# A stored order of work replaced by a newly searched one, with 80 identity products in place of 120

## The chip, the core and the metric

The kernel runs on one core of one Trainium2 chip. The metric is the device time of one launch in microseconds (us). The kernel before has a median of 756.46 us over 3 runs (756.37 to 758.33). TensorE (PE in the rows) multiplies matrices and writes PSUM, VectorE (DVE), ScalarE (ACT) and GpSimd (POOL) work on elements, SyncE (SP) issues DMAs. GpSimd doesn't read PSUM in this kernel: all its operands lie in SBUF.

## The reference

Three networks follow each other; the weights of the last two come as float64.

```
q_assign = argmax(q_n . c_n); k_assign = argmax(k_n . c_n)        # 16 clusters, per head
scores = where(q_assign == k_assign, q k^T / 8, -1e9)             # 2 x 8 heads x 768 x 768
x = softmax(scores) v                                             # to 1536 tokens x 512
h = x @ w_in;  g = h if h >= 1, 0 if h <= -1, else (h+1)^2/4;  x = g @ w_out
out = ((x @ w1) * (x @ w2)) @ w3 @ w_out2
```

## The kernel before

**Stages.** The 1536 tokens are two blocks, one a batch. A block has 4 units (pairs of heads), a unit two halves of 384 queries, a half six scores: 96 scores, s 0 to s 95, each of 128 queries by 768 keys. For a score TensorE multiplies twice into a buffer of PSUM (`s_mm`, line 799: the parts, then the mask); VectorE takes the maximum (line 807), GpSimd scales it (812), ScalarE exponentiates (820). Every score of block 0 and every third of block 1 is then transposed on TensorE (837), the others by DMA. Only when ScalarE and VectorE have copied the result out, or split it into high and low parts (lines 348 to 353), is the PSUM buffer free. After six scores `pv` multiplies with v into the one bank `av` (908, 916), VectorE scales the result there (927, 929) and splits it into X.

While attention runs, float64 weights are turned into floats: ScalarE (1051, 1080), VectorE (1055, 1061, 1067, 1073), GpSimd (1084). w3 and w_out2 are multiplied to one matrix (`wp_mm`, 1142). The dense layers of block 0 (`mm4`, 1198; twelve products of 128x384 a step) run between the scores of block 1; those of block 1 come last, partly by products of quarter matrices (1450). Block 0's scores use four PSUM buffers, block 1's two.

**What sets the order.** Every step is entered in a plan with `add(name, {engine: cost}, due, fn, needs, takes, frees, ..., near)`. `Plan.order` doesn't search: it reads the table `ORDER`, two letters a step, which give the step's number and which of its engines does it, and issues the steps so. Costs, due times and `near` steer only the search that once made the table, which isn't in the file. Each engine executes its instructions in that order and waits by semaphores for tiles. `needs` are only asserted on.

**The identity products.** `idle_mm` (line 460) multiplies the identity matrix with itself into columns 384 to 511 of the bank `av`; nobody reads them. As a writer of the tile `av`, such a product waits for earlier readers of `av`, which later serves as a bank of the dense layers too. There are 120: `N_IDLE` = 90 that come after `c_const`, which makes the identity, and `N_IDLE1` = 30 that come after score 47, the last of block 0. In TensorE's order 50 of them stand ahead of the first score, 21 between the first and the seventh, 49 after the seventh.

**The start.** The centroids are loaded and normed (lines 413 to 442); TensorE multiplies k and q with them (512); VectorE makes masks in four steps, for k and for q (526, 532, 539, 544), TensorE (548) and VectorE (552) end them, and a DMA on ScalarE's queue carries the mask to the first score. Meanwhile q and k are split: high parts on ScalarE or VectorE, low parts (`q_lo`, `k_lo`, line 353) on GpSimd or VectorE.

Of the kernel before, what the change touches and what calls it, by code (L numbers as in the profile page):

```python
# [38 lines left out]
    "###%#*#,#6#(#<#8#:#@#.#0%u(.&y(<#F#D%w(D%y#2%|&#&%&(&*&,&2&|(P(#(0(4(2(,&4(F&8&6(H<8#J#N#L#a#B#_#e#i#X&:&<&>"  # L39
    "&@&B#y$(&.#o#|#m$,#s#c#H$%$6$>#u(>(@&0#4#k&D&F(8<F<:<R((<<(%<a(6(J<H<J<><@(*<T<V<L<N(:<m<B<D(B<c(L$:$H#R#P$R"  # L40
    "#q#Z$F$L$J$_$a$##g$]$D$X$*$m+@+B<]<P=#=2<o+X+D+L+N+P+R+e+g+i+k+F<q<X+Z<e+]<g<Z<i<_$N%#%*%%$q$V$0$Z$e$k$4%(#]"
    "$.$w+T+m+H+K=%+_+a$u%.%6$T=4=6<k=8+V+c+q+s$@$<,#,@=:=<=@=L+o+u+w<w=>,%,(,B,D$o#w$B%2$y$8$P,L$2+y%0,*+|,,,.(N"
    "=(<s=*=,<u=.=0<y$s%4$|,X,Z,](c,N,P,0,2,e,8=B=D=F=N=P=H=R=J=T,F,H=Z,_,R,T$i=g=w(T(V,4,7#T,J,V,q,g,i=V=X=]=i,s"
    ",a-#-%-(,u<|,d,:(^(k(n=_=k(S=m=a,k>0,w,y>@-*(_,<(b,>=o-0,m,o,|-,$g-@$c#V-X-L-Z-.-8=q=s-2-B-D-]=y(Z>2(X-F-e-H"
    "-N-P-R-_=|>4>#>%=c&H>(>*(s-J>:>6=e>8><-T-a-V-c>N>B>_-q-g-i-s-u-k=u>,>.-w>D>F>H>J>L.#.@.B-4-6>q-:.%>P>R-m-y>>"
    "?(?6.(.D>T>V(j>X>Z-o-|.*.0.F.2.L.X.N.P.Z.]>a>c?F-<>e->>s?*.,.H...R.J._>u(r>g?,>w?.>i>k&J).?0?2?4(y(|>]>m>o.e"
    "(e(g?X.T.a.g.i>y(v.4(x.7>|?#.V)%.c?8?@(o.8),/#.q.k.m?i#>?%/%/(?w)(.o.s.u.w/*?:?<?>?B/@/B/D?H?J?Z?k)6/F)#?]?m"
    "?o.:.<?L?N.>/,.y.|/.&L?D?c?T?V)*/H)0/0/2?q?s?P?u?R/L/N/P/R?_?a/K)8?e)4@(@.):?y/8)3/T/4/7/X/Z/]/:/</q/e/g)@/_"
    "/i/s/u@@@P/k/w?g/W?|@#@%@*@0)<@_@B/a0#@o0%0(0*/y/m/o/c@D@2@4@6@F@H@8@:/|@J@L@,@=/>0@0,0B&c&a@>0X0L@i@R@T@V)D"
    ")J)FA(0.@N08@a0D0F0H0N0Z0]0P)M@c)C)Q&e)H&N@X@q0R0_0aA*&g)R%,0T@e@g00@Z@]@s@u@w@yA,@|0JA.A0@k&PA2A402A80V0c)N"  # L50
    "AFAV0e0g0i&R&T0k&i&k&V&mA:A<&o@mA#)>0m0o0q04Ai06Ay0s0u0w0:0<1#1%1(AH1*&qA>A@&XABADAJ0>ALANA60y&s1,0|1.&Z1@1L"
    "1NA%&u&wAPAXAkAZ1P&]&_18B.1RARB>A|1B1D1F10121X1Z1]AmAoA]A_AaAcB#AqB%1_ATAeAg)XB(B*B,1H1T1aAsAu1J1V1c1e1q1sBP"
    "B81416B01g1i1u1wBa1k1:B2B4B6B:2@2#2B2%2(AwB@BR2*20222D1y1m1o1~1<2FBoB<BL)T)V2,2HBBBD1>BFBHBTBN)ZBJ2.BZBVBXB]"
    "2L2N2PBcC%2JByBeBgBiBkBm2RBqBsBuBw2426282T2V2e2X2Z2g2q3#)_B|2i2k2]2_2s2u3%)])h)b)c3(2:)qB_2m)f)jC(GX2w3*3032"
    "2<2>C*)nC,C.C02oC#C4C8CV2y2a2c3,2|3.)sC2C6)l)o34363N%a3PC:C<3R3TCu3V3@3B3D3F)u)w383:CYD:3=3X3>CZ)y)|C>C@CC3H"
    "3J3Z3LCwDX*#CyCDCFDw3]3_3aCJCLCOCH3k3mD<CPCS3c3e3g3iC]C_E<CT3o3qD>CbCcCiCk3y3|4#CeCgEJ3s3u3w4%CnCoCrCs4(4*C|"
    "D#D%D(D.DZDyGuD0D24.4042D]4446D+D,D4D6D@DB4J4L4N4P*%4,484:*(DLDED8D~DFDIDJ4XDNE>E@DQ4R4T4VDRDkDm4<4>DoDqEXD_"
    "4Z4g4iELDaDT**EgEuDd4]4kDVDtDu4_H64a*-*/*04c4eEODe4m4o4qDgDi4s4DEBEDE#E%E)4u4w4y4|E*E-E.E0E2EZE]5*5,5.*2E4E6"
    "5#5%5(4@EFE8F:5052EHE:4C5456585:5<Ei*5*?*@*6*85>*:5@FXGc5B5DH@EcEeE_5c5e5g5i5kEkET5T5V5XEb5F*B5HEPEwEz5mFwF<"
    "EVG<5ZEqEmEREsEoF?4FF[4H*<F^5J5q5s5u*D5]5_5aGJGZG]5MG_GaE|F.FzF|F#F%F(F+6%6(6*5o5w5y5|6#F0GwF2F4GyF7F,G|H#F8"  # L60
# [24 lines left out]
    "]q^u_6]#]4_D^w[o]%[u^C^0]n^D]7]>_F_*]s^o^k]@]B]*],]v_-_8`V].]8];]<^m_L_N^y]0]2_Q]f]E_#^%_I_%]F_;`X_T_J_R[q^q"
# [56 lines left out]
def cluster_attention_moe_kernel(  # L142
# [200 lines left out]
    def f(t):  # L343
        return t.bitcast(F32)
# [298 lines left out]
    def by_copy(u):  # L643
        return u < NP
# [1071 lines left out]
```

## Time and profile before

| | |
|---|---|
| median of 3 runs | 756.46 us |
| profiled execution | 756.23 us |
| its span, first to last instruction | 754.5 us |
| around the span | 1.7 us |
| TensorE, VectorE, ScalarE, GpSimd busy | 97%, 85%, 59%, 40% of the span |
| granted TensorE clock, mean | 0.997 |

The busy shares say which engine has no room left. The granted clock is a share of 2.4 GHz, and 0.5 of it is 1.2 GHz. In a timeline, an idle time in brackets with a name after the arrow is a wait of that engine and who ended it. A record of a matrix product lasts longer than the distance to the next one, since products overlap in the pipeline: what a product costs is read from start to start. Plain float32 products have two records each, so line 460 has 240 records.

### The profile page before, as it was taken

How to read it: one execution, taken by the hardware profiler on the slowest of the kernel's cores; microseconds unless marked ns; L12 is line 12 of the kernel's file. 1: busy time of each engine (PE TensorE's matmuls, PEld its weight loads, DVE VectorE, ACT ScalarE, POOL GpSimd, SP SyncE). 2: the span in 40 equal slices, each digit the busy share in tenths (PEclk: the TensorE clock that was granted, in tenths of full speed). 3: DMA queues.
4: the chain of work that ended last, by engine and by line, in shares of the span. 5: the costliest groups of instructions: out<-in, count | busy, mean ns of one | idle time of the engine just before them, and what ended most of it. 6: DMA issues, size and time to landing. Idle time of an engine off the chain costs nothing.

```text
span 754.5 us, 12341 instructions
## 1 busy us (share of the span) xinstructions
PE 729.9 (97%) x4352; PEld 646.8 (86%) x4353; DVE 638.7 (85%) x1148; ACT 446.8 (59%) x832; POOL 303.0 (40%) x367
## 2 busy tenths in 40 slices
PE   6998999999999999999998999999999999999998
PEld 4975656556599999998998999999899999999997
DVE  5998888988888889999999999759898888899841
ACT  6687887667777867695775665422664444443310
POOL 6242244222343424454354422225561543167711
PEclk9999999999999999999999999999999999999999
DMA  8463565756668767697877785453231303122212
GB/s 291 124 204 111 177 206 201 265 185 200 178 163 190 141 157 189 177 238 192 215 167 204 198 221 148 119 186 120 63 99 29 99 28 99 56 58 69 63 55 92
DMA packets 100973, 112.77 MB, mean 149 GB/s; under 512 B 61488, under 2 KB 69680, under 8 KB 100912
## 3 DMA queue, kind: packets, MB, share of 16 engines
q1 hardware_dynamic: 78768, 52.48, 27.4%
q10 hardware_dynamic: 22144, 59.52, 25.2%
q8 instruction: 34, 0.56, 0.3%
q14 instruction: 27, 0.22, 0.1%
HBM read 73.70 MB, written 20.19 MB: 124 GB/s over the span
## 4 chain that ended last, share of the span: by engine, by line
PE 76%; DVE 13%; ACT 4%; issue 3%; DMA 3%; POOL 0%; ACTq 0%; DVEq 0%; POOLq 0%
PE mo L1198 33%; PE sc L799 7%; PE sc L1450 6%; PE sc L1198 6%; PE mo L1142 4%; PE mo L1450 4%; PE sc L837 4%; PE av L460 3%; PE av L916 3%; PE av L908 2%; PE av L1450 2%; DVE nm L807 2%; DVE wf L1055 1%; ACT pt L348 1%; DVE wf L1067 1%
## 5 line engine op out<-in xcount | busy, mean ns | idle before, releaser
L1198 PE MATMUL mo<-X,whl 128*128 128x384 f32 x900 | 168.8, 341 | 0.0
L1198 PEld LDWEIGHTS mo<-X,whl 128*128 128x128 f32 x900 | 157.2, 190 | 2.0 <-ACT P L820 0.6
L1198 PE MATMUL mo<-G,whl 128*128 128x384 f32 x720 | 133.2, 339 | 0.0
L353 POOL TENSOR_TENSOR whl<-wf,whl 128x512 fp32r<-128x512 f32 x60 | 80.3, 1339 | 130.5 <-ACT whl L348 73.6
L1198 PEld LDWEIGHTS mo<-G,whl 128*128 128x128 f32 x720 | 125.4, 188 | 1.5 <-DVE kq L350 0.3
L807 DVE TENSOR_REDUCE nm<-sc 128x1 f32<-128x768 f32 x96 | 89.8, 950 | 19.2 <-PE sc L799 15.6
L1084 POOL TENSOR_TENSOR wf<-wf,w 128x512 int32<-128x512 int32 x32 | 43.1, 1347 | 74.3 <-ACT w L1080 23.0
L820 ACT ACTIVATE P<-sc,nm 128x768 f32<-128x768 f32 x64 | 57.4, 899 | 23.4 <-POOL nm L812 14.7
L812 POOL TENSOR_SCALAR nm<-nm 128x1 f32<-128x1 f32 x96 | 23.9, 249 | 111.8 <-DVE nm L807 106.3
L799 PE MATMUL sc<-k,q 128*128 128x512 f32 (+1 forms) x192 | 55.2, 369 | 5.9 <-DVE phl L353 4.1
L348 ACT ACTIVATE whl<-wf 128x512 fp32r<-128x512 f32 x70 | 43.7, 627 | 25.5 <-PE mo L1198 9.6
L348 ACT ACTIVATE pt<-sc 128x768 f32<-128x768 f32 (+1 forms) x59 | 46.3, 808 | 20.1 <-PE sc L837 16.0
L1142 PE MATMUL mo<-wo,wf 128*128 128x512 f32 x128 | 57.7, 593 | 0.0
L837 PEld LDWEIGHTS sc<-ident,P 128*128 128x128 f32 x384 | 43.6, 141 | 11.5 <-ACT P L820 5.3
L837 PE MATMUL sc<-ident,P 128*128 128x128 f32 x384 | 49.8, 274 | 2.4 <-ACT P L820 2.3
L799 PE MATMUL sc<-kq 80*128 80x512 f32 (+1 forms) x192 | 49.5, 339 | 0.0
L1051 ACT ACTIVATE wf<-w 128x512 f32<-128x512 f32 x64 | 42.6, 674 | 8.0 <-POOL wf L1084 2.3
L1067 DVE SCALAR_TENSOR_TENSOR wf<-w,wf 128x512 uint32<-128x512 uint32 x64 | 44.1, 691 | 1.2
L1142 PEld LDWEIGHTS mo<-wo,wf 128*128 128x128 f32 x128 | 23.5, 190 | 23.7 <-issue 23.1
L799 PEld LDWEIGHTS sc<-k,q 128*128 128x128 f32 x192 | 31.6, 189 | 14.0 <-DVE phl L353 4.6
L460 PE MATMUL av<-ident 128*128 128x128 f32 x240 | 36.9, 287 | 6.7 <-DVE X L353 2.6
L460 PEld LDWEIGHTS av<-ident 128*128 128x128 f32 x240 | 33.5, 199 | 10.0 <-DVE X L353 2.9
(218 smaller groups left out, 1537.1 us busy)
## 6 DMA issues: line engine op xcount, KB each, us to landing
wf<-wd ACTq DMA_DIRECT2D x64, 256.0 KB, 2.7
w<-in_w_out_dram ACTq DMA_DIRECT2D x24, 512.0 KB, 4.2
wd<-wf SPq DMA_DIRECT2D x48, 256.0 KB, 3.0
w<-in_w3T_dram ACTq DMA_DIRECT2D x16, 512.0 KB, 4.1
w<-in_w_in_dram ACTq DMA_DIRECT2D x16, 512.0 KB, 4.8
w<-in_w_dram ACTq DMA_DIRECT2D x16, 512.0 KB, 4.1
wf<-wp ACTq DMA_DIRECT2D x16, 256.0 KB, 3.1
kq<-in_kT_dram SPq DMA_DIRECT2D x8, 384.0 KB, 5.1
```

The source lines that it names most:

```text
L348: nc.scalar.activation(out=out, in_=in_, func=AF.Copy)
L353: (nc.gpsimd if e == "POOL" else nc.vector).tensor_tensor(out=out, in0=a, in1=b, op=ALU.subtract)
L460: nc.tensor.matmul(BUFS["av"][0][:, TG:TG + 128], ident, ident, start=True, stop=True)
L799: nc.tensor.matmul(ps[:, n], q[0:n_rows, q0:q0 + 128], k[0:n_rows, n], start=first, stop=not first)
L807: nc.vector.tensor_reduce(out=nm, in_=T[("sc", b), s], axis=AX.X, op=ALU.max, negate=True)
L820: nc.scalar.activation(out=new(("P", b), s).rearrange("p n s -> p (n s)") if by_pe(s) else T[("sc", b), s], in_=T[("sc", b), s], func=AF.E ...
L837: nc.tensor.transpose(T[("sc", b), s][:, c], p[:, c], ident)
L1067: nc.vector.scalar_tensor_tensor(out=w, in0=T[w64, i][:, :, 1], scalar=0xC0000000, in1=w, op0=ALU.bitwise_and, op1=ALU.bitwise_or)
L1084: nc.gpsimd.tensor_tensor(out=w, in0=w, in1=T[w64, i].bitcast(I32)[:, :, 0], op=ALU.add)
L1142: nc.tensor.matmul(acc, w[:, k4 * 128:(k4 + 1) * 128], wo2[:, hf * 4 + k4], start=(hf == 0 and k4 == 0), stop=(hf == 1 and k4 == 3),)
L1198: nc.tensor.matmul(acc, w[:, a, k4 * 128:(k4 + 1) * 128], rhs(c, k4), start=(first and k4 == 0 and n == 0), stop=(last and k4 == 3 and n = ...
L1450: nc.tensor.matmul(ps, lhs(av, a, k), rhs(bv, c, k), start=k == 0 and n == 0, stop=k == 1 and n == 2,)
```

## The change

The table is replaced (3134 steps become 3094). The entries that steered the search change with it:

```diff
-    "###%#*#,#6#(#<#8#:#@#.#0%u(.&y(<#F#D%w(D%y#2%|&#&%&(&*&,&2&|(P(#(0(4(2(,&4(F&8&6(H<8#J#N#L#a#B#_#e#i#X&:&<&>"
...
+    "##%%%(%*%:#*#,#%#8#(#4%#%@%>%<#<#@#B&*#.#0#2&8&-#L%,&(&>&;&F&7&D#c#P;@&0#R#6#a;N;Z;i%.#:#k%B&N&P&@#Z$(;J%0%2"
...
-        plan.add(name, engines, due, fn, needs, takes, frees, behind, moves, (near if near and near[0] == ("sc", 0) else None))
+        plan.add(name, engines, due, fn, needs, takes, frees, behind, moves, (near if near and near[0] in (("sc", 0), "av") else None))
...
-    N_IDLE, N_IDLE1 = 90, 30
+    N_IDLE, N_IDLE1 = 80, 0
...
-            add(("idle", after, i), {"PE": 0.22}, 1e4 + i, idle_mm, [(lag + 0.23 * i, after)])
+            add(("idle", after, i), {"PE": 0.22}, 1e4 + i, idle_mm, [(lag + 0.23 * i, after)], near=("av", "cT"))
...
-            add(("am", b, w), {"PE": 1.8}, t + 0.9, a_mm(b, w, range(NP)), ...
+            add(("am", b, w), {"PE": 1.8 if b else 2.4}, t + 0.9, a_mm(b, w, range(NP)), ...
...
-                    [("k2", u, h), ("klo", u, h)] + ([("k2h", u, h), ("q1h", u, h)] + ...
+                    [("k2", u, h), ("klo", u, h)] + ([("idle", "c_const", i) for i in range(N_IDLE)] if s == 6 else []) + ([("k2h", u, h), ("q1h", u, h)] + ...
```

The remaining lines of the diff add `near=` for the bank `av` to `c_T`, `c_put`, the splits of X, `pv` and `xm`. Since the table alone is read, what changes on the chip is the order, the engines of some steps, and 40 products fewer. The table is a line shorter, so code behind it moves up a line: line 799 of before is 798 in the change.

Of the 80 products 50 stand ahead of the first score, 30 between the first and the seventh, none after (before: 50, 21, 49). VectorE has 1112 steps (1107 before), ScalarE 897 (893), GpSimd 345 (354). Counted in the order, VectorE has 390 steps ahead of the maximum of score 66 (378 before) and 591 ahead of that of score 84 (576).

VectorE at the start, before, from the making of k's mask on (`sc` is a PSUM buffer, `P` and `phl` its tiles for masks):

```order
L526 STREAM_TRANSPOSE P_106<-sc_175 128x768
L532 TENSOR_REDUCE amx<-P_106 128x48
L539 TENSOR_TENSOR phl_108<-P_106,amx 128x768
L544 STREAM_TRANSPOSE phl_108<-phl_108 128x768
L526 STREAM_TRANSPOSE P_107<-sc_175 128x768
L532 TENSOR_REDUCE amx<-P_107 128x48
L539 TENSOR_TENSOR phl_109<-P_107,amx 128x768
L544 STREAM_TRANSPOSE phl_109<-phl_109 128x768
L552 TENSOR_SCALAR mask_115<-sc_176 128x768
L552 TENSOR_SCALAR mask_115<-sc_175 128x768
```

and in the change, from the second of two low parts of q on:

```order
L352 TENSOR_TENSOR q_100<-kq_116,kq_103 64x768
L349 CAST k_97<-kq_116 64x768
L525 STREAM_TRANSPOSE P_106<-sc_177 128x768
L531 TENSOR_REDUCE amx<-P_106 128x48
L538 TENSOR_TENSOR phl_108<-P_106,amx 128x768
L543 STREAM_TRANSPOSE phl_108<-phl_108 128x768
L525 STREAM_TRANSPOSE P_107<-sc_177 128x768
L551 TENSOR_SCALAR mask_115<-sc_178 128x768
L531 TENSOR_REDUCE amx<-P_107 128x48
L538 TENSOR_TENSOR phl_109<-P_107,amx 128x768
L543 STREAM_TRANSPOSE phl_109<-phl_109 128x768
L551 TENSOR_SCALAR mask_115<-sc_177 128x768
```

VectorE now does two low parts of q (which GpSimd did) and a high part of k (which ScalarE did) ahead of the masks; and it ends k's mask (L551) ahead of three steps of q's.

TensorE around scores 12 and 14, before (`P` are exponentials that are transposed, `k`, `q` and `kq` a score's operands):

```order
L837 MATMUL sc_175<-ident,P_107 128x128 x6
L460 MATMUL av<-ident 128x128
L799 MATMUL sc_175<-k_98,q_101 128x256
L799 MATMUL sc_175<-k_98,q_101 128x512
L799 MATMUL sc_175<-kq_104 128x256
L799 MATMUL sc_175<-kq_104 128x512
L460 MATMUL av<-ident 128x128 x2
L799 MATMUL sc_176<-k_98,q_101 128x512
```

and in the change:

```order
L836 MATMUL sc_177<-ident,P_107 128x128 x6
L798 MATMUL sc_177<-k_98,q_101 128x256
L798 MATMUL sc_177<-k_98,q_101 128x512
L798 MATMUL sc_177<-kq_104 128x256
L798 MATMUL sc_177<-kq_104 128x512
L798 MATMUL sc_178<-k_98,q_101 128x512
L798 MATMUL sc_178<-k_98,q_101 128x256
L798 MATMUL sc_178<-kq_104 128x512
```

The scores follow the transposes without an identity product between them.

TensorE around score 83 (into buffer `sc_1768`), before; the next score into the same buffer, 84, begins with the last row (`mo` are banks of the dense layer):

```order
L799 MATMUL sc_1768<-kq_103 128x512
L799 MATMUL sc_1768<-kq_103 128x256
L799 MATMUL sc_1767<-k_96,q_99 128x512
L799 MATMUL sc_1767<-k_96,q_99 128x256
L799 MATMUL sc_1767<-kq_102 128x512
L799 MATMUL sc_1767<-kq_102 128x256
L1198 MATMUL mo_1762<-X_1861,whl 128x384 x12
L1198 MATMUL mo_1763<-X_1861,whl 128x384 x12
L1198 MATMUL mo_122<-X_1861,whl 128x384 x12
L460 MATMUL av<-ident 128x128
L799 MATMUL sc_1768<-k_96,q_99 128x512
```

and in the change, where that buffer is `sc_1746` and score 84 follows behind the last row:

```order
L798 MATMUL sc_1746<-kq_103 128x512
L798 MATMUL sc_1746<-kq_103 128x256
L1198 MATMUL mo_122<-X_1888,whl 128x384 x12
L1198 MATMUL mo_1740<-X_1888,whl 128x384 x12
L1198 MATMUL mo_1741<-X_1888,whl 128x384 x12
L798 MATMUL sc_1745<-k_96,q_99 128x512
L798 MATMUL sc_1745<-k_96,q_99 128x256
L798 MATMUL sc_1745<-kq_102 128x512
L798 MATMUL sc_1745<-kq_102 128x256
L1198 MATMUL mo_122<-X_1888,whl 128x384 x12
L1198 MATMUL mo_1740<-X_1888,whl 128x384 x12
L1198 MATMUL mo_1741<-X_1888,whl 128x384 x12
```

Between the two scores into one buffer stood three dense steps, score 85 and an identity product; now six dense steps and score 85. On VectorE, 8 steps stand between score 83's maximum and the low part that frees its buffer before, 16 in the change.

## Rows read from the trace of the kernel before

**Rows 1.** the page's first part: busy us (share of the span) xinstructions by engine.

```profile
PE 729.9 (97%) x4352; PEld 646.8 (86%) x4353; DVE 638.7 (85%) x1148; ACT 446.8 (59%) x832; POOL 303.0 (40%) x367
```

**Rows 2.** waits of TensorE by releaser: us in total, times, longest.

```profile
PE sc L799 <- DVE phl L353: 4.1, 2, 2.7
PE av L460 <- DVE X L353: 2.6, 1, 2.6
...
PE av L460 <- ACT tmp L1617: 1.6, 1, 1.6
...
PE av L460 <- DVE G L350: 1.0, 1, 1.0
```

**Rows 3.** line 460 alone by stretch: busy us (xrecords, two a product), clock, DMA.

```profile
38.80:64.00 25.20, 5.20 (x34) 4.41 (x34) 1.00 0.54 175
64.00:754.50 690.50, 12.29 (x64) 10.65 (x64) 1.00 0.53 145
```

**Rows 4.** TensorE's timeline, 22 to 27 us: start, us, instruction.

```profile
22.26 4.41 PE L460 MATMUL av<-ident 128*128 128x128 f32 x38
26.42 0.60 PE L799 MATMUL sc<-k,q 128*128 128x256 f32 x2
```

**Rows 5.** the same view, 297.8 to 299 us: one product before another shape.

```profile
297.80 0.39 PE L460 MATMUL av<-ident 128*128 128x128 f32 x2
297.94 1.31 PE L1198 MATMUL mo<-G,whl 128*128 128x384 f32 x6
```

**Rows 6.** the same view, 56 to 62 us.

```profile
56.70 2.13 PE L837 MATMUL sc<-ident,P 128*128 128x128 f32 x18
61.46 0.49 PE L460 MATMUL av<-ident 128*128 128x128 f32 x2 [2.63 <-DVE X L353]
```

**Rows 7.** VectorE's timeline, 404 to 414 us.

```profile
404.79 0.94 DVE L807 TENSOR_REDUCE nm<-sc 128x1 f32<-128x768 f32 x1
...
407.06 1.49 DVE L1055 TENSOR_SCALAR wf<-wf 128x512 f32<-128x512 f32 x1 [0.52 <-issue]
408.58 1.95 DVE L1061 TENSOR_SCALAR wf<-wf 128x512 uint32<-128x512 uint32 x1
...
413.23 0.95 DVE L353 TENSOR_TENSOR phl<-sc,phl 128x768 f16<-128x768 f32 x1
```

**Rows 8.** GpSimd's timeline, 406 to 411 us.

```profile
406.97 1.29 POOL L353 TENSOR_TENSOR whl<-wf,whl 128x512 fp32r<-128x512 f32 x1 [0.96 <-ACT wf L1051]
408.34 1.90 POOL L353 TENSOR_TENSOR k<-raw,k 64x768 fp32r<-64x768 f32 x1
```

**Rows 9.** TensorE's timeline, 404 to 415 us.

```profile
404.84 6.46 PE L1198 MATMUL mo<-X,whl 128*128 128x384 f32 x36
...
414.23 0.62 PE L799 MATMUL sc<-k,q 128*128 128x512 f32 x2 [2.71 <-DVE phl L353]
```

**Rows 10.** all engines by stretch: busy us (xinstructions), granted clock PEclk, DMA share, GB/s.

```profile
415.20:418.60 3.40, 3.40 (x12) 3.40 (x12) 3.33 (x5) 3.35 (x7) 1.32 (x1) 0.51 0.63 189
418.60:422.00 3.40, 3.40 (x21) 3.40 (x21) 3.12 (x7) 2.70 (x6) 1.50 (x2) 0.99 1.01 222
```

**Rows 11.** the same view, long stretches.

```profile
0.00:26.40 26.40, 19.13 (x143) 14.98 (x144) 17.60 (x34) 15.80 (x21) 13.03 (x17) 1.00 0.67 223
26.40:300.00 273.60, 266.82 (x1550) 201.13 (x1550) 239.56 (x391) 209.34 (x369) 96.78 (x134) 1.00 0.64 184
300.00:450.00 150.00, 145.86 (x919) 137.60 (x918) 142.22 (x241) 101.39 (x185) 63.25 (x69) 0.99 0.77 200
```

**Rows 12.** VectorE's timeline, 12 to 25 us.

```profile
12.84 0.98 DVE L526 STREAM_TRANSPOSE P<-sc 128x768 f32<-128x768 f32 x1 [2.86 <-PE sc L512]
...
20.88 0.98 DVE L544 STREAM_TRANSPOSE phl<-phl 128x768 bf16<-128x768 bf16 x1
21.78 1.78 DVE L552 TENSOR_SCALAR mask<-sc 128x768 fp32r<-128x768 f32 x2
...
24.15 0.42 DVE L1061 TENSOR_SCALAR wo<-wo 128x512 uint32<-128x512 uint32 x1
```

More of the change, by code (lines that the diff above doesn't have):

```diff
@@ L44 @@
[L44 to L48, printed above, removed]
@@ L98 @@
+    "j@k1k2k4k:j|jBk7k=jVjXk>k8jqjsju"
 )
@@ L583, in cluster_attention_moe_kernel @@
                 )
-            add(("am", b, w), {"PE": 1.8}, t + 0.9, a_mm(b, w, range(NP)), ["c_put"] + [("al", b, w, x) for x in range(NP)], [(("sc", 0), ("a", b, w))], near=(("sc", 0), ("a", b, w)))
+            add(("am", b, w), {"PE": 1.8 if b else 2.4}, t + 0.9, a_mm(b, w, range(NP)), ["c_put"] + [("al", b, w, x) for x in range(NP)], [(("sc", 0), ("a", b, w))], near=(("sc", 0), ("a", b, w)))
             steps = [("DVE", 0.92), ("DVE", 0.88), ("DVE", 0.9), ("DVE", 0.92), ("PE", 0.28), ("DVE", 0.88)]
@@ L950, in add_split @@
             hi, lo = {"ACT": 0.41, "DVE": (0.27, LATE)}, {"POOL": 0.97, "DVE": (0.47, LATE)}
-        add((key + "h",) + name[1:], hi, t, split_hi(tile, dst), needs)
-        add((key + "l",) + name[1:], lo, t + 0.5, split_lo(tile, dst), [(key + "h",) + name[1:]], frees=[tile])
+        near = tile if ring == "av" else None
+        add((key + "h",) + name[1:], hi, t, split_hi(tile, dst), needs, near=near)
+        add((key + "l",) + name[1:], lo, t + 0.5, split_lo(tile, dst), [(key + "h",) + name[1:]], frees=[tile], near=near)
     def to_dram(name, dst):
@@ L971, in cluster_attention_moe_kernel @@
                     ("s", s), {"PE": 0.7}, p, s_mm(s, u, g, h, t),
-                    [("k2", u, h), ("klo", u, h)] + ([("k2h", u, h), ("q1h", u, h)] + ([("qh0", u)] if h else []) if by_copy(u) else []),
+                    [("k2", u, h), ("klo", u, h)] + ([("idle", "c_const", i) for i in range(N_IDLE)] if s == 6 else []) + ([("k2h", u, h), ("q1h", u, h)] + ([("qh0", u)] if h else []) if by_copy(u) else []),
                     [(("sc", b), s)],
@@ L1011, in cluster_attention_moe_kernel @@
                 ("pv", u, g), {"PE": 4.17 if whole(u) else 3.24}, p, pv(u, g), [("vT", u)] + [("sT", s + r) for r in range(NS)],
[L1012 removed]
+                [("av", (u, g))], [("pt", (u, g, 0)), ("pt", (u, g, 1))] + ([("vn", u)] if g == NG - 1 else []), near=("av", (u, g)),
             )
             nm = ("x", u, g)
[L1015 removed]
+            add(("xm", u, g), {"DVE": 0.5}, p + 3.0, x_mul(u, g), [("pv", u, g), ("ri", u, g)], [("tmp", nm)] if b else [], [("av", (u, g)), ("rb", (u, g))] if b else [("rb", (u, g))], near=("av", (u, g)))
             if b == 0:
```

115 lines of the change are left out of this document (58 added, 57 removed).

## The prediction, as it stood before the result was known

> **What bounds the kernel now.** Read the busy shares first: TensorE is busy for 729.9 of 754.5 us, no other engine over 85% [rows 1]. So the time is TensorE's own work plus what it waits, and a change helps if it takes work from TensorE or shortens waits there. Next the waits by releaser: the longest sums behind the start are scores that wait for a low part on VectorE (4.1 us in two waits), and, oddly, identity products that wait: 2.6, 1.6 and 1.0 us [rows 2]. They compute nothing and yet stand in TensorE's way. Third, the busy time in long stretches: VectorE is at 239.56 of 273.6 us (88%) from 26.4 to 300 and at 142.22 of 150 (95%) from 300 to 450 [rows 11]. It's the engine that could become the next limit.
>
> The sum is made against the profiled execution, 756.23 us (754.5 of span and 1.7 around it), 0.2 us under the median.
>
> **The 49 late products go.** The records of line 460 behind 38.8 us are 34 and 64, two a product, so 17 and 32 products [rows 3]. In a row of 19, 38 records take from 22.26 to 26.42, that is 0.22 us a product [rows 4]; a single one before another shape delays the next instruction by 0.14 [rows 5]. So 49 cost between 6.9 and 10.8 us where nothing else is waited for. Part of the first 17 stand in rows, most of the 32 alone: I take 8.7. It is nothing where the next instruction would have waited anyway, and that is the danger below.
>
> **Their own waits go.** A product writes the bank `av`. The one at 61.46 us waited 2.63 us for VectorE to read that bank out, with the transposes before it over at 58.8 [rows 6]. The instruction behind it is a score, which goes to another bank. The change puts scores there straight behind transposes. With those of 1.6 and 1.0 us [rows 2] this is 5.2; I take 5.0, since the next instruction may have had some wait of its own.
>
> **Nine products are added between the first and the seventh score** (30 for 21). At 0.22 each [rows 4] that's 2.0 us, or nothing if TensorE would wait for exponentials there. I take 2.0.
>
> **The start.** Two low parts of q and a high part of k move to VectorE, in front of the masks. VectorE sits idle for 2.86 us there until the products with the centroids end [rows 12]; three such steps, at up to 0.95 each, fill that and cost nothing, provided that q arrives in time (its load moves up one place on SyncE's queue, ahead of the first k). k's mask is ended ahead of three of q's steps. One of the two masks takes 0.89 (1.78 for both) [rows 12], so q's last transpose ends that much later, at 22.7 in place of 21.86; behind it come TensorE's step of q and 18 identity products of 0.22 [rows 4]. The first score then starts near 27.0 instead of 26.42: I take 0.6 us. It could be 0, or 1.5 if the low parts come late.
>
> **The long wait at 414 us.** Score 84 waited 2.71 us [rows 9] for the low part of score 83, which shares its buffer. Score 83's maximum began at 404.79, its low part ended at 414.18 [rows 7]: 9.4 us for 10 steps, which at VectorE's mean of 0.61 (239.56 us for 391 instructions [rows 11]) are 6.1. Where did the rest go? Two instructions of 128x512 took 1.49 and 1.95 us, while the second kind takes 0.42 elsewhere [rows 7, 12]; GpSimd had operations of 1.29 and 1.90 us at those very times [rows 8]. The two engines get in each other's way in SBUF, some 2.6 us here. TensorE had only three dense steps of 2.15 (6.46 for three [rows 9]), a score and an identity product to fill the time. In the change six dense steps and a score stand there, 13.6 us, and VectorE has 18 steps, 11.0 us. A stall as large as the old one would use that up exactly. So I let the wait go: 2.7 us. Behind it the granted clock fell to 0.51 for 3.4 us, which is the 1.2 GHz level, and 12 products ran where the next 3.4 us had 21 [rows 10]: about 1.7 us lost. Both terms together are 4.4, and 0 if something else is late there.
>
> **What is late next.** TensorE comes earlier, the other engines have the same work. Up to 300 us the order gives VectorE 12 more steps (390 for 378 ahead of score 66's maximum). Three lie in the idle time of the start; nine are 5.5 us at 0.61, in a stretch shortened from 273.6 to some 265: 92% busy in place of 88%. From 300 to 450 us, at 95%, TensorE waits for 4.1 of 150 us, 2.8%; from 26.4 to 300 for 6.8, of which 2.6 is an identity product's, so 4.2 or 1.5% [rows 6, 11]. If the first stretch came to wait like the second, that's 7.5 us in 265, 3.3 more. I take 3.5 (bounds 0 and 10, about all that is saved there). From 300 to 450 us I don't count the 2.0 us of some 14 products that go, since VectorE at 95% sets the pace. Behind 450 VectorE has room, and the change has less for it at the end: nothing.
>
> **Sum.** 756.2 - 8.7 - 5.0 + 2.0 + 0.6 - 4.4 + 3.5 + 2.0 = 746.2.
>
> **Rivals.**
>
> A. VectorE becomes the bound and eats half. For it: 15 more steps ahead of score 84's maximum (591 for 576), 9.2 us at 0.61, of which only the 2.5 of the start are covered; the stretch after 300 is at 95% [rows 11]. Against it: VectorE still idles 34 us from 26.4 to 300 [rows 11], and its stalls behind GpSimd may shrink. Time: the sum without the wait at 414 and without the two terms of lateness is 745.1; plus 6.7 gives 751.8.
>
> B. The change doesn't do what it says: the engines collide as often as before, and only the products' absence counts. For it: GpSimd keeps nearly all its steps (345 of 354). Time: 745.1 + 3.5 + 2.0 = 750.6.
>
> C. Slower: block 1's scores have two buffers, so each waits for the low part of the second score before it. Two such waits exist, 4.1 us [rows 2], and the new order sets other distances at all 46. At 1.5 us a late release, 8 of them take back 11.1 and from there the kernel is slower; 12 give 763. Against it: the distance grows where the largest wait is, and only two were late before.
>
> D. The clock. The granted clock fell once behind a wait of 2.71 us, and not behind one of 2.63 [rows 6, 9, 10]. Without the products TensorE may stand still more often; two falls at 1.7 us added to the sum give 749.6. The Trainium skill's page "TensorE: Matmul & The Clock Gate", Part 1, says that the clock follows how busy TensorE has been and that the half rate is where it stands by default; by it, taking out filler speaks against this change. The trace agrees so far as the one fall stands behind the longest wait; by the page the sum would be this rival's 749.6 if two waits grow to that length, and 746.2 if none does.
>
> E. Better than the sum: no new lateness, early products hidden. 756.2 - 8.7 - 5.2 + 0.6 - 4.4 = 738.5.
>
> **Chances.** Forecast 0.50 (its own range 741 to 751), A 0.20, B 0.12, C 0.08, D 0.05, E 0.05. The range to quote, 740 to 755, takes in A, B and D, most of the forecast's bounds and leaves out C and E with some edges. A difference of 0.3%, 2.3 us, is what a measurement of this kernel can tell. Faster than that: all of the forecast and E, 0.13 of A, 0.11 of B, 0.04 of D: 0.83. Within it: 0.06 of A and 0.01 each of B, C and D: 0.09. Slower: 0.07 of C, 0.01 of A: 0.08.
>
> **What would show it.** TensorE's busy time falls by about 8 us, and line 460 keeps 160 records, all ahead of some 42 us; no wait of line 459 (460 before) behind the start. The first score starts at 26.4 to 27.5 and score 12 near 58, 3 to 4 us sooner than at 61.7, right behind the product of [rows 6]. No wait over 1 us at the score that corresponds to the one at 414, and the clock at 1.00 around it. VectorE's 128x512 operations have fewer instructions over 1 us. The prediction is wrong if TensorE's idle time behind the start, 17.3 us before (754.5 - 729.9 [rows 1] less 7.3 up to 26.4 us [rows 11]), grows by as much as its busy time falls; then A or C holds, and the waits name VectorE, in the first 300 us (A) or at scores of block 1 (C).

## The result, and the profile after

| | us, median (lowest to highest) | profiled execution: time, span |
|---|---|---|
| before | 756.41 (754.21 to 758.33) | 756.23, 754.5 |
| after | 737.08 (736.46 to 738.52) | 738.52, 736.8 |

The ratio is 0.9748, 95% interval 0.9718 to 0.9778: 19.3 us faster, where 10.2 were forecast. The profiled execution of after is the slowest of its four. The kernel after has line numbers one less up to 908, and the same from 1055 on.

The first part of the page, as in [rows 1], busy us by engine:

```profile
PE 721.2 (98%) x4273; PEld 638.4 (87%) x4273; DVE 629.2 (85%) x1153; ACT 445.2 (60%) x836; POOL 284.0 (39%) x358
```

TensorE's busy time fell by 8.7 us and its idle time from 24.6 (754.5 - 729.9) to 15.6 (736.8 - 721.2), by 9.0. Together that is the 17.7 us of the span. Waits of TensorE by releaser, answering [rows 2]: us in total, times, longest.

```profile
PE av L436 <- DVE P L432: 3.1, 1, 3.1
PE sc L836 <- ACT P L819: 2.2, 1, 2.2
PE sc L798 <- ACT pt L347: 2.1, 3, 1.6
PE av L459 <- POOL ident masks.py:199: 1.4, 1, 1.4
...
PE av L459 <- DVE cT L441: 0.6, 1, 0.6
```

No score waits for a low part any more (4.1 us before), and the two waits of identity products that are left belong to the start. The busy time by long stretch, answering [rows 11]:

```profile
0.00:26.40 26.40, 19.65 (x139) 15.07 (x140) 18.66 (x37) 16.21 (x22) 9.41 (x14) 1.00 0.73 257
26.40:300.00 273.60, 268.90 (x1544) 203.03 (x1543) 241.73 (x403) 202.78 (x363) 92.81 (x132) 0.99 0.66 182
300.00:450.00 150.00, 150.00 (x957) 141.50 (x957) 143.49 (x259) 110.41 (x201) 65.22 (x75) 1.00 0.86 211
```

From 300 to 450 us TensorE does not idle at all (4.1 us before), and VectorE, though only 1.3 us more busy, ended 259 instructions where it had ended 241. That is the row to stop at: 18 more instructions at the 0.61 us of the prediction would be 11.0 us, and the busy time has 1.3 of them. Most of the rest came out of the instructions' own durations. VectorE's two kinds of 128x512 operations on one input in this stretch (count | busy us, mean ns | idle before), before:

```profile
L1055 DVE TENSOR_SCALAR wf<-wf 128x512 f32<-128x512 f32 x23 | 14.9, 660 | 1.4 <-ACT wf L1051 0.7 <-issue 0.5
...
L1061 DVE TENSOR_SCALAR wf<-wf 128x512 uint32<-128x512 uint32 x23 | 13.2, 577 | 0.3
```

and after:

```profile
L1061 DVE TENSOR_SCALAR wf<-wf 128x512 uint32<-128x512 uint32 x25 | 12.0, 479 | 0.3
L1055 DVE TENSOR_SCALAR wf<-wf 128x512 f32<-128x512 f32 x25 | 10.7, 434 | 0.0
```

Undisturbed, one takes 0.42 us [rows 12]. Above that there were (0.660 - 0.42 + 0.577 - 0.42) x 23 = 9.1 us of stalls in these two lines before, and 1.8 after. Before, eight of these instructions took 1.38 to 1.95 us. Each began while a GpSimd operation of 128x512 or 64x768 ran and ended 0.28 or 0.29 us after it, as the two of [rows 7] do behind the two of [rows 8]. After, the longest takes 1.09 us, though GpSimd is no less busy there (65.2 us, 63.3 before): the two engines' operations meet less often. Why this table makes them meet less isn't shown.

From 26.4 to 300 us other lines of VectorE had stalled. Two of them, before and after:

```profile
L1073 DVE SCALAR_TENSOR_TENSOR wf<-w,wf 128x512 uint32<-128x512 uint32 x18 | 15.1, 844 | 0.3
...
L1067 DVE SCALAR_TENSOR_TENSOR wo<-w,wo 128x512 uint32<-128x512 uint32 x7 | 6.3, 916 | 0.0
```

```profile
L1073 DVE SCALAR_TENSOR_TENSOR wf<-w,wf 128x512 uint32<-128x512 uint32 x18 | 12.4, 686 | 0.3
...
L1067 DVE SCALAR_TENSOR_TENSOR wo<-w,wo 128x512 uint32<-128x512 uint32 x7 | 4.7, 688 | 0.1
```

That is (0.844 - 0.686) x 18 + (0.916 - 0.688) x 7 = 4.4 us less for the same 25 instructions.

Line 459 by stretch, answering [rows 3]: all 160 records, two a product, lie ahead of 45 us.

```profile
0.00:45.00 45.00, 22.46 (x160) 20.82 (x160) 1.00 0.59 205
45.00:736.80 691.80, 0.00 (x0) 0.00 (x0) 1.00 0.56 150
```

TensorE's timeline at three places: the first score (26.42 before [rows 4]), score 12 (61.7 before), and the score that waited at 414 us [rows 9], now at 407.63 behind two blocks of three dense steps and score 85:

```profile
22.90 4.18 PE L459 MATMUL av<-ident 128*128 128x128 f32 x36
26.84 0.36 PE L798 MATMUL sc<-k,q 128*128 128x256 f32 x1
...
57.19 2.13 PE L836 MATMUL sc<-ident,P 128*128 128x128 f32 x18
59.07 0.60 PE L798 MATMUL sc<-k,q 128*128 128x256 f32 x2
...
401.27 6.52 PE L1198 MATMUL mo<-X,whl 128*128 128x384 f32 x36
407.63 0.51 PE L798 MATMUL sc<-k,q 128*128 128x512 f32 x2
```

One new wait came, at 214 us: transposes of a score on TensorE wait for an exponential on ScalarE, which itself came 3.5 us late because a transpose by DMA of the probabilities took 9.75 us. The granted clock is at 0.50, the 1.2 GHz level, in the stretch behind it:

```profile
214.61 1.00 PE L836 MATMUL sc<-ident,P 128*128 128x128 f32 x6 [2.17 <-ACT P L819]
```

```profile
211.80:215.20 3.40, 1.23 (x9) 0.92 (x8) 1.52 (x2) 2.81 (x6) 0.82 (x1) 1.00 1.18 289
215.20:218.60 3.40, 3.40 (x13) 3.21 (x12) 3.25 (x6) 2.81 (x6) 2.29 (x3) 0.50 0.64 122
218.60:222.00 3.40, 3.40 (x20) 3.36 (x20) 3.35 (x6) 2.81 (x7) 1.29 (x1) 1.00 0.00 0
```

### The profile page after: what moved, and what is told of

It reads as the page before. It is cut to its first block, busy times and chain, and to the rows that moved or that the text cites. A ratio compares the mean times of both kernels' runs of the same rounds, so it can differ in the third digit from the quotient of the medians.

```text
span 736.8 us, 12150 instructions
## 1 busy us (share of the span) xinstructions
PE 721.2 (98%) x4273; PEld 638.4 (87%) x4273; DVE 629.2 (85%) x1153; ACT 445.2 (60%) x836; POOL 284.0 (39%) x358
## 4 chain that ended last, share of the span: by engine, by line
PE 76%; DVE 2%; DMA 2%; ACT 2%; issue 0%; POOL 0%; ACTq 0%; DVEq 0%
PE mo L1198 35%; PE sc L1450 7%; PE sc L1198 7%; PE sc L798 6%; PE mo L1450 6%; PE av L915 3%; PE mo L1142 3%; PE sc L836 3%; PE av L1450 2%; PE av L1198 1%; DMA pt<-phl 1%; PE av L907 1%; PE mo L893 1%; ACT P L819 0%; DMA wd<-wf 0%; DMA wf<-wd 0%
## 5 line engine op out<-in xcount | busy, mean ns | idle before, releaser
L1198 PE MATMUL mo<-X,whl 128*128 128x384 f32 x900 | 165.8, 339 | 0.0
L1198 PE MATMUL mo<-G,whl 128*128 128x384 f32 x660 | 121.6, 337 | 0.0
L1198 PEld LDWEIGHTS mo<-G,whl 128*128 128x128 f32 x660 | 114.9, 188 | 1.1 <-DVE wf L1061 0.3
L352 POOL TENSOR_TENSOR whl<-wf,whl 128x512 fp32r<-128x512 f32 x54 | 70.7, 1312 | 74.2 <-DVE whl L349 38.0
L347 ACT ACTIVATE pt<-sc 128x768 f32<-128x768 f32 (+1 forms) x53 | 41.8, 808 | 20.4 <-PE sc L836 16.7
L1198 PE MATMUL sc<-G,whl 128*128 128x384 f32 x252 | 46.0, 337 | 0.0
L1198 PEld LDWEIGHTS sc<-G,whl 128*128 128x128 f32 x252 | 44.2, 188 | 0.0
L352 POOL TENSOR_TENSOR wh<-ws,wh 128x256 fp32r<-128x256 f32 x44 | 33.5, 775 | 18.0 <-DVE wh L349 7.6
```

Source lines behind the costliest of these rows:

```text
L347: nc.scalar.activation(out=out, in_=in_, func=AF.Copy)
L352: (nc.gpsimd if e == "POOL" else nc.vector).tensor_tensor(out=out, in0=a, in1=b, op=ALU.subtract)
L1198: nc.tensor.matmul(acc, w[:, a, k4 * 128:(k4 + 1) * 128], rhs(c, k4), start=(first and k4 == 0 and n == 0), stop=(last and k4 == 3 and n = ...
```

## The experiments

"Old order" is the kernel before, "new order" the one after. Each is the kernel named with only the edit shown or told, most of them in the loop that issues the steps. A median stands beside the ratio to the kernel before, measured alongside on the same chip, with its 95% interval.

**Products and order apart.** Old order without the late products:

```
+  if name[0] == "idle":
+      products += 1
+      if products > 71: continue        # the 49 behind the seventh score
```

> The kernel before with its own order, without the 49 identity products behind the seventh score; the 71 early ones stay. Theory 1 (the sum's terms are right and do not depend on the order): the products cost 8.7 us and their own waits 5.0, so about 742.5 to 743.5 us, and the difference to the changed kernel's 737.1 is what the new order itself gives. Theory 2 (VectorE sets the pace in the old order): TensorE's other waits grow by more than half of what goes, 748 to 752 us. Theory 3 (the filler keeps the clock up): falls of the granted clock to 0.5 appear and the time is 750 or more.

New order with them, in front of the same steps of TensorE:

```
+  for _ in range(late.get(name, 0)): idle_mm("PE")     # 49 in all
```

> The changed kernel with 49 identity products put back, each row of them in front of the same step of TensorE as in the kernel before. Theory 1 (costs add, whatever the order): 8.7 us of products and up to 5 of waits for the bank, so 746 to 751 us. Theory 2 (in the new order they fall into waits): under 741 us.

| | with the 49 late products | without | products |
|---|---|---|---|
| old order | 756.4 | 747.5 (ratio 0.9882, 0.9860 to 0.9903) | -8.9 |
| new order | 747.0 (0.9874, 0.9850 to 0.9898) | 737.1 | -9.9 |
| order | -9.4 | -10.4 | |

By the intervals each difference is good to 2 or 3 us. Half the gain is the order's, which the prediction had as a loss (2.0 + 0.6 - 4.4 + 3.5 + 2.0 = +3.7). And in the old order the products cost their work and, on balance, no waits: TensorE's idle time was 24.6 us with them and 25.1 without. Its longest waits without, and its busy time up to 300 us:

```profile
PE sc L837 <- ACT P L820: 5.4, 5, 3.1
PE sc L799 <- DVE phl L353: 4.9, 3, 2.9
```

```profile
0.00:26.40 26.40, 19.76 (x142) 15.50 (x143) 17.67 (x34) 15.77 (x21) 13.00 (x17) 1.00 0.66 224
26.40:300.00 273.60, 265.46 (x1519) 198.66 (x1519) 242.13 (x395) 210.24 (x372) 98.92 (x135) 1.00 0.64 186
```

These two waits were 2.3 and 4.1 us with the products. The three waits of identity products (5.3 us) are gone, and about as much came at other places: 2.0 us for exponentials at 40 to 57 us, 3.05 us in place of 1.30 at 165 us, 0.8 more for low parts, 1.2 at two dense products (372 and 672 us). TensorE comes sooner and waits later.

**The three products that waited** [rows 2], taken out of the old order alone (`if name in three: continue`).

> The kernel before without the three identity products that waited 2.63, 1.64 and 1.03 us for readers of the bank av. Theory 1 (these waits are pure loss): 5.3 us and 0.7 for the products themselves, 750.4 us, and the three waits are gone from the trace without others over 1 us in their places. Theory 2 (the steps behind them would have waited too): within 2 us of before, 754 to 756.5.

751.75 us (0.9927, 0.9902 to 0.9952), 4.2 less, between the two theories. Another product then waits at nearly the same place,

```profile
61.20 0.71 PE L460 MATMUL av<-ident 128*128 128x128 f32 x4 [1.93 <-DVE X L353]
```

and behind it the clock falls to 0.50 for 3.4 us. A wait of 2.63 us was removed, 1.93 came back; of the other two (1.64 and 1.03) 0.66 came back, at 678 us.

**The early products.** New order without the 30 between the first and the seventh score, then without all 80:

```
+  if name[0] == "idle": products += 1; if products > 50: continue
```

> The changed kernel without the 30 identity products between the first and the seventh score; the 50 ahead of the first stay. Theory 1 (they lie in waits for exponentials): 736 to 738 us, and TensorE idles there instead. Theory 2 (half of them delay the scores, as the prediction's term of 2.0 us has it): 733 to 735.5 us. Theory 3 (they keep the clock up): a fall to 0.5 between 27 and 45 us and 738 to 740 us.

737.92 us (0.9755, 0.9731 to 0.9779): the same as after. The 30 lie in waits for exponentials, which show as waits instead.

```
+  if name[0] == "idle": continue
```

> The changed kernel without any of the 80 identity products. Theory 1 (the start is set by the chain over centroids and masks, the products fill waits): 735.5 to 737.5 us. Theory 2 (without them TensorE's clock is at 1.2 GHz when the first products and scores run): the granted clock is 0.5 up to some 30 us, the products with the centroids take up to twice as long, 738 to 742 us.

743.34 us (0.9833, 0.9810 to 0.9856), 6.3 slower than after. The first scores start earlier (23.85 for 26.84 us) but run slower; the same two products of an early score there and in the kernel after:

```profile
28.62 0.84 PE L798 MATMUL sc<-kq 80*128 80x512 f32 x2
```

```profile
28.35 0.51 PE L798 MATMUL sc<-kq 80*128 80x512 f32 x2
```

From start to start these two take 0.64 us for 0.36, about what the lower clock would make; the clock itself isn't recorded before 32 us in that trace. At score 12 the kernel stands 2.1 us behind the one after. Another 3.0 us go at 371 us, where TensorE waits 2.28 us for an exponential; no run ties that wait to the start.

**Does VectorE set the pace?** In the new order six maxima of scores between 300 and 450 us are computed twice (5.2 us more on VectorE, nothing else):

```
+  if name in [("smax", s) for s in (69, 73, 77, 81, 85, 88)]:
+      nc.vector.tensor_reduce(out=small("twice"), in_=T[("sc", 1), name[1]], axis=AX.X, op=ALU.max, negate=True)
```

> The changed kernel with six score maxima taken twice on VectorE (scores 69, 73, 77, 81, 85 and 88; 0.87 us each from start to start, 5.2 us more work between 300 and 450 us, where VectorE is busy for 143.5 of 150 us). Theory 1 (VectorE's occupancy sets the pace there, as the prediction's term for lateness has it): 741 to 742.3 us and waits of TensorE for VectorE between 300 and 450 us. Theory 2 (the order leaves TensorE's work enough ahead, so that occupancy costs nothing until it is full): 737 to 738.8 us and at most 1.5 us of waits there.

742.50 us (0.9822, 0.9798 to 0.9846): 5.4 us for 5.2. VectorE's whole busy time rose by 6.3 us (629.2 to 635.5), 1.1 more than was added. TensorE's idle time there goes from 0 to 2.5 us, and its score of 420.5 us starts 4.3 us later:

```profile
300.00:450.00 150.00, 147.50 (x925) 137.63 (x924) 146.79 (x258) 106.20 (x193) 61.42 (x71) 1.00 0.81 205
```

So in this stretch a microsecond of VectorE's is about a microsecond of the time. The next one was to bring the stalls back: in the new order 64 multiplications of 128x128 on GpSimd, four behind each of 16 scalings there.

> The changed kernel with 64 small GpSimd multiplications of 128x128 in SBUF, four behind the scaling of each of 16 scores' maxima from 68 to 90, results unused; GpSimd is busy for 65 of 150 us between 300 and 450 us, so it has room. Theory 1 (the two engines hold each other up in SBUF, and the new order gained by avoiding it): VectorE's busy time in that stretch grows by 3 us or more for about the same instructions, TensorE waits again for low parts, 739.5 to 745 us. Theory 2 (GpSimd's use of SBUF is no matter, the gain is from the distances between steps): VectorE's mean duration is unchanged, 736.5 to 738.5 us.

745.41 us (0.9861, 0.9835 to 0.9887), 8.3 slower, and VectorE 5.3 us more busy with the same 1153 instructions. But TensorE also waits for GpSimd itself (4.6 us in four waits), so this run doesn't tell the two apart.

**One GpSimd instruction moved.** The 1.90 us operation of [rows 8] beside which VectorE's 1.95 us one ran. The first try changed nothing: no other step of GpSimd's stood between the old place and the new, so its order stayed. The second moved it behind the scaling of score 85.

```
+  if name == ("klo", 7, 1): held = fn, e; continue
   fn(e)
+  if name == ("slo", 83): held[0](held[1])        # second run: ("sbias", 85)
```

> The kernel before, with one GpSimd operation (the low part of k that ran at 408.3 us for 1.90) issued behind the low part of score 83 and not ahead of it. Theory 1 (GpSimd's use of SBUF held VectorE's instruction at 408.58 for 1.5 us, and through it score 84): that instruction takes 0.42 instead of 1.95 us, the wait at 414 us shrinks from 2.71 to about 1.2, and the clock does not fall behind it: 753 us, 3.2 less. Theory 2 (VectorE was late for its own work): the wait stays over 2.3 us and the time within 1 us of before.

755.73 us (0.9995, 0.9981 to 1.0009): it says nothing on the theories, since nothing was moved.

> The old order with one GpSimd instruction moved: the 64x768 subtraction of the seventh head's keys (1.90 us, from 406.97 us), now behind the scaling of score 85, so behind the place where two of VectorE's 128x512 operations ended in 1.49 and 1.95 us beside it. Theory of the stalls: those two end in about 0.42 us if nothing else of GpSimd runs there, the wait of score 84 (2.71 us) falls to 0.5 to 1.5 us, the clock stays at its upper level at 415 us, and the time falls by 2 to 4 us, to 752 to 754. Rival (score 84 is late for where it stands in the order): the wait and the time stay, 755 to 757.

755.18 us (0.9984, 0.9971 to 0.9998). VectorE and the score, answering [rows 7, 9]:

```profile
407.40 1.49 DVE L1055 TENSOR_SCALAR wf<-wf 128x512 f32<-128x512 f32 x1 [0.53 <-issue]
408.92 0.43 DVE L1061 TENSOR_SCALAR wf<-wf 128x512 uint32<-128x512 uint32 x1
```

```profile
413.06 0.62 PE L799 MATMUL sc<-k,q 128*128 128x512 f32 x2 [1.19 <-DVE phl L353]
```

Line 1061 went from 1.95 to 0.43 and the wait from 2.71 to 1.19 us: the same 1.52 us. Line 1055 kept its 1.49 beside the 128x512 operation that had stayed. The clock didn't fall, and the 36 dense products behind the score took 6.52 us for 8.00; before, and then in this run:

```profile
415.03 8.00 PE L1198 MATMUL mo<-X,whl 128*128 128x384 f32 x36
```

```profile
413.86 6.52 PE L1198 MATMUL mo<-X,whl 128*128 128x384 f32 x36
```

Wait and clock are 3.0 us together. Of these 2.0 are left at score 86 (0.41 of the rest went to transposes that now wait for an exponential); it starts 1.7 us earlier than before, since the run was 0.3 us late up to here. Of the time 1.2 us (0.2 to 2.2) is seen by the ratio, less than expected.

**The stalls taken out of the old order.** From score 69 to score 92 GpSimd's two kinds of 128x512 operations keep their place and lose 7/8 of their columns; the kernel leaves out the rest of the weights' low parts, so its output is not the reference's. The old order has all its 120 products here (80 in the expectation is a slip).

```
-  sub(e, w[:, 1], T["wf", i], f(w)[:, 0])
+  sub(e, w[:, 1, :64], T["wf", i][:, :64], f(w)[:, 0, :64])     # on GpSimd; products read w[:, 0]
-  nc.gpsimd.tensor_tensor(out=w, in0=w, in1=lo, op=ALU.add)
+  nc.gpsimd.tensor_tensor(out=w[:, :64], in0=w[:, :64], in1=lo[:, :64], op=ALU.add)
```

> The old order with all its 80 products; from score 69 (310 us) to score 92 (461 us) GpSimd's subtractions that make the low halves of the weights and its additions of the low words go over 64 columns instead of 512, and the products that would read those low halves read the high halves instead (that part of the output is left out). Every instruction stays, on its engine and in its place. In the kernel before, VectorE had ten stalls of 0.24 to 1.53 us (9.6 us) in this stretch, about 6.7 us of them beside these GpSimd operations alone. Theory (the order's gain is the stalls that it takes from VectorE, and VectorE sets the pace there): these stalls go, and the time falls by 5 to 7 us, to 749 to 751. Rival (the gain is in the sequence itself, how early scores and dense steps stand to each other; the stalls lie in slack): 754 to 756.

> The same cut in the new order, where VectorE's stalls in the stretch are 1.9 us in all. Theory of the stalls: little is left to gain, 735.5 to 737. Rival (the cut helps as shorter GpSimd work in itself, not by VectorE's stalls): as much as in the old order, 730 to 732.

758.38 us in the old order (1.0034, 1.0019 to 1.0048) and 739.51 in the new (0.9781, 0.9757 to 0.9806). By the time the theory had failed: slower, where 5 to 7 us were expected. The trace says more. Score 76 stood 0.9 us behind that of the kernel before (a difference from ahead of the cut), score 86 was 4.4 us ahead: 5.3 us gained. Then ScalarE waited 6.9 us for a weight's load, TensorE 5.5 for what hangs on it, and the clock fell. In the new order nothing was gained in the stretch (score 68 was 1.6 us behind the kernel after, score 94 1.7). The theory has it so, but TensorE doesn't idle there in any case, so no theory would have shown a gain. What it lost lies ahead of the cut, at a wait of 1.9 us for a transpose by DMA.

The cut was made again without the late products, up to score 86 and up to 92.

> The old order without its 49 late products, and GpSimd's two kinds of 128x512 operations cut to 64 columns from score 69 up to score 86 (the low halves are left out of these products). Without the cut that order takes 747.5 us, and TensorE idles 6.0 us from 350 to 450 us. Theory of the stalls: VectorE's 128x512 operations of 1.5 us are down to 0.4 us there, TensorE idles 1 to 2 us in 350 to 450, and the time falls to 742 to 744. Rival (the sequence): the idle time and the time stay, 746.5 to 748.

> The same, with the cut up to score 92. Theory of the stalls: 741 to 743, if no transpose and load meet as in the run before; if they do (a wait of ScalarE for a weight load above 4 us), 747 to 750. Rival (the sequence): 746.5 to 748.

749.55 (0.9928, 0.9906 to 0.9950) and 749.97 us (0.9930, 0.9913 to 0.9946), both over the 747.5 without the cut. Again score 86 came sooner (from score 76 to it 5.6 and 5.4 us gained) and a load took it back. SyncE's and ScalarE's queue in the first of them, and the wait:

```profile
407.65 1.93 SPq L869 DMA_TRANSPOSE pt<-phl  x1
409.67 0.88 SPq L679 DMA_DIRECT2D raw<-in_vT_dram  x1
...
411.13 2.68 SPq L869 DMA_TRANSPOSE pt<-phl  x1
```

```profile
412.18 0.33 ACTq L1044 DMA_DIRECT2D w<-in_w_dram  x1
...
424.59 0.66 ACT L1053 ACTIVATE wf<-w 128x512 f32<-128x512 f32 x1 [7.83 <-DMA w<-in_w_dram]
```

What was issued from 410 to 428 us there, KB each, median us to landing:

```profile
w<-in_w_dram ACTq DMA_DIRECT2D x2, 512.0 KB, 12.2
...
pt<-phl SPq DMA_TRANSPOSE x1, 13.6
```

That transpose isn't needed before 459 us. So it was issued later, once with the cut and once, as a control, without:

```
+  if name == ("sT", 85): held = fn, e; continue
   fn(e)
+  if name == ("wd", 40): held[0](held[1])
```

> The old order without its 49 late products, GpSimd's 128x512 operations cut to 64 columns from score 69 to score 86, as before, and the transpose of score 85's probabilities (not needed before 459 us) issued behind the store of weight 40 instead of ahead of it, so some 3 us later and away from the transpose before it. Theory of the stalls: the weight load takes 4 to 6 us, no wait of TensorE above 2 us in 420 to 435 us, and the time falls from 747.5 to 741 to 744. Rival (the sequence sets the pace, and the gain up to score 86 is given back in any case): 746.5 to 749.

> The old order without its 49 late products and with the transpose of score 85's probabilities issued behind the store of weight 40; GpSimd's operations whole. If the gain of the run before came from VectorE's stalls: 747 to 748.5, as without the move, and TensorE still idles about 6 us from 350 to 450 us. If it came from the transpose: 741 to 744.

741.61 us with the cut (0.9816, 0.9793 to 0.9839), 748.38 without (0.9891, 0.9871 to 0.9910). With the cut that is 5.9 us under the old order without late products (5.0 by the ratios), without it no gain. The stretch from 300 to 450 us of the old order without late products, then with the cut and the move, then with the move alone:

```profile
300.00:450.00 150.00, 144.00 (x902) 134.01 (x902) 143.63 (x245) 103.51 (x189) 63.67 (x70) 1.00 0.77 202
```

```profile
300.00:450.00 150.00, 148.33 (x931) 138.84 (x931) 141.79 (x254) 105.28 (x191) 43.34 (x73) 1.00 0.80 207
```

```profile
300.00:450.00 150.00, 143.38 (x893) 132.65 (x892) 142.14 (x242) 102.24 (x186) 63.54 (x70) 1.00 0.77 201
```

TensorE's idle time falls from 6.0 to 1.7 us with the cut and is 6.6 with the move alone. VectorE's two lines without the cut, then with cut and move (0.42 to 0.44 us each, 7.4 us of stalls gone):

```profile
L1055 DVE TENSOR_SCALAR wf<-wf 128x512 f32<-128x512 f32 x23 | 13.9, 613 | 1.4 <-ACT wf L1051 0.7 <-issue 0.5
L1061 DVE TENSOR_SCALAR wf<-wf 128x512 uint32<-128x512 uint32 x22 | 12.8, 584 | 0.3
```

```profile
L1057 DVE TENSOR_SCALAR wf<-wf 128x512 f32<-128x512 f32 x24 | 10.3, 439 | 1.6 <-ACT wf L1053 1.1 <-issue 0.4
L1063 DVE TENSOR_SCALAR wf<-wf 128x512 uint32<-128x512 uint32 x24 | 10.2, 427 | 0.3
```

Of the 4.9 us of scores waiting for a low part 1.4 are left. TensorE's busy time is the same (719.6 us in both), so it is waits that went: 5.8 us of idle time in these two profiles, 4.3 of them in this stretch and 1.4 ahead of the cut, where the two differ without it. A rival is that shorter GpSimd work helps in itself, by scaling the maxima sooner. The rows speak against it: without the cut TensorE waited here for low parts from VectorE and only 0.2 us for exponentials, and with it VectorE idled no less (8.2 us for 6.4) but ended 254 instructions for 245.

**A version beyond both.** The new order with three loads issued behind the transposes that they had slowed down at 203 to 212 us:

```
+  held = {("ul", 5, "k"): ("sT", 52), ("wl", 44): ("sexp", 50), ("wl", 45): ("sexp", 50)}   # step: issued behind
```

> The new order with three loads issued later: the sixth head's keys (384 KB) behind the transpose of score 52 instead of ahead of the transposes of 50 to 52, and the weights 44 and 45 (256 KB each) behind the exponential of score 50. In the new order a transpose of the probabilities takes 9.75 us beside these loads, ScalarE waits 3.5 us for it, TensorE 2.2 us for ScalarE at 214 us, and the clock falls for 3.4 us behind that. Theory: the transpose takes 5 to 7 us, the wait and the fall of the clock go, and the time falls by 2 to 4 us, to 733 to 735. Rival (VectorE paces this stretch too, so the wait only moves to the next score): 736.5 to 737.5.

> The changed kernel itself, beside the version with later loads on one chip: 736.5 to 738.

> The new order with the three loads issued later, as before. If its gain is real: 733.5 to 735.5, 2 to 4 us below the changed kernel in the same call, with no wait above 1 us of TensorE from 200 to 300 us. If not: within 1 us of it.

734.75 us (0.9730, 0.9706 to 0.9754), and a second time, beside the changed kernel on one chip, 734.88 (0.9739, 0.9720 to 0.9758) against 736.79 (0.9764, 0.9746 to 0.9782). The two transposes there, one of which had taken 9.75 us, now have a median of 5.1, and the wait at 214 us is gone:

```profile
207.99 4.33 PE L1198 MATMUL mo<-X,whl 128*128 128x384 f32 x24
212.16 0.82 PE L836 MATMUL sc<-ident,P 128*128 128x128 f32 x6
```

It is some 2 us lower both times, but the intervals overlap, so the gain is likely and not certain. The changed kernel itself doesn't always pay: in its second profile the wait there was 1.2 us and the clock stayed up.

## Why the prediction was wrong

The direction was right and the size wrong: 737.1 us lies below the range, 740 to 755. Point by point:

- **The late products (-8.7): right.** The terms of TensorE's busy time come to -8.7 + 2.0 for the nine early products - 1.7 for the clock = -8.4; it fell by 8.7.
- **Their own waits (-5.0): gone in the new order, but not a gain by themselves.** In the old order without the products TensorE's idle time stayed at 25.1 us: what these waits gave back was waited elsewhere. The products' absence brought 8.9 to 9.9 us in all, not 13.7.
- **Nine early products (+2.0): 0.** Without any of the 30 the time is the same. The seventh score came 2.8 us later, score 12 was ahead again by 2.6; both were seen in the timeline.
- **The start (+0.6): right,** 0.42 us at the first score.
- **The wait at 414 us (-4.4): right in kind.** No wait, and the clock at 1.00 in all of 300 to 450 us. The moved GpSimd operation showed the mechanism on one instruction: 1.52 us off VectorE, 1.52 off the wait, and 1.5 for the clock where 1.7 were forecast; but of these 3.0 us 2.0 were left at score 86, so the two don't simply add.
- **What is late next (+3.5 and +2.0): the step that failed.** The prediction let the other engines have the same work: up to 300 us nine more steps for VectorE at 0.61 us, so 92% busy and more waits of TensorE, and from 300 to 450 us a VectorE at 95% that gives nothing back. It had the stalls beside GpSimd in hand at one place, 2.6 us, and used them for that one wait; it expected fewer long instructions, and gave them no term. In the old order without the late products the feared lateness did come (5.3 us of waits gone, idle time unchanged). In the new order VectorE's work got shorter instead: 9.1 us of stalls in two lines from 300 to 450 us became 1.8, and two other lines lost 4.4 us from 26.4 to 300, where VectorE ended 403 instructions for 391 and was 88% busy (241.73 of 273.6 us) as before. So TensorE waits less there, not more. Idle time of TensorE by stretch, us, from the rows above and [rows 11] (the old order without late products has the same products as the new one but for nine early ones):

| | 0 to 26.4 | 26.4 to 300 | 300 to 450 | behind | all |
|---|---|---|---|---|---|
| before | 7.3 | 6.8 | 4.1 | 6.4 | 24.6 |
| old order, no late products | 6.6 | 8.1 | 6.0 | 4.3 | 25.1 |
| after | 6.8 | 4.7 | 0.0 | 4.1 | 15.6 |

The forecast's idle terms come to -5.0 - 2.7 + 0.6 + 3.5 + 2.0 = -1.6; it was -9.0. That difference of 7.4 us is nearly all of the 7.7 us by which the profiled execution (738.5) lies under the forecast of 746.2; the median lies 9.1 under it.

What is shown: VectorE's time from 300 to 450 us sets the pace (5.4 us for 5.2 added), and without its stalls the old order is 5.9 us faster, with a control that isn't. What is argued: that the other 3.4 us of idle time that the order saves, from 26.4 to 300 us, go back to the same cause. The stalls fell there too, by 4.4 us in two lines, but no run touched that stretch. The old order without late products and stalls (741.6) still lies 4.5 us above the new one; what the choice of an engine for each step and the sequence bring to that wasn't tried apart.

The Trainium skill's page "GPSIMD Engine Reference", Specifications, says that GpSimd shares its SBUF interfaces with VectorE and that VectorE's instructions with two SBUF inputs, or with one in a 2-port mode, contend. The trace agrees that the two engines hold each other up (1.95 us and 0.43 for one and the same instruction, with and without a GpSimd operation beside it). That instruction has one input; whether it ran in a 2-port mode no row tells.

Of the rivals, A (VectorE as the bound) had the right engine and the wrong sign, B (as many collisions) and C (block 1's buffers) fell: no score of block 1 waits for a low part. D's clock fell once in the middle, behind the new wait at 214 us, as it had at 415: one fall for one, so nothing was lost by it. E, no new lateness and the early products hidden, came nearest with 738.5 and had been given 0.05.

## What to carry to other kernels

Where an engine is at 95% of its time, look first at how long its instructions take beside how long the same form takes elsewhere: stalls are counted as busy, and an estimate that takes the busy time over takes them over. A change that removes such stalls gives time back where that engine releases what the bound engine waits for: in the old order 5.9 us for 7.4, once nothing else stood in the way. And a wait removed from filler work counts only as far as the steps that then come sooner don't wait later: with three products gone 4.2 us were gained, with all 49 gone TensorE's idle time stayed.

## What the runs showed that was not expected

- Filler at the start pays: without all 80 identity products the first scores started 3.0 us earlier, ran slower (0.84 us for 0.51) and the kernel was 6.3 us slower, of which the trace shows some 2 by score 12; 30 of them between the scores cost nothing.
- Transposes by DMA and loads can slow each other by far more than their sizes say. With the cut and the move a transpose of one score's probabilities landed in 4.2 us, and the two 512 KB loads issued behind it took 5.2. Without the move the next transpose was issued 3.5 us behind the first, and the two loads behind it: it took 13.6 us and they 12.2. What the other transpose and the loads each do to it no run separates. In three runs that took back 5.3 to 5.6 us which had been gained on VectorE; a gain can be there in the trace up to one place and not in the time.
- A wait's length alone doesn't tell whether the clock falls. Behind a wait of 2.17 us at 214 us and one of 2.71 at 414 us the granted clock was at half for 3.4 us. Behind 2.93 us at 411 us and 3.05 us at 165 us, in the old order without late products, it stayed at 1.00.
